# Moving one batch's loads and row tiles in a tuned attention and feed-forward kernel

## The chip, the cores and the metric

The kernel runs on one core of one Trainium2 chip. The metric is device time in microseconds (us), the median of several executions. Engines: PE is TensorE's matmul stream, PEld its weight loads, DVE is VectorE, ACT is ScalarE, POOL is GpSimd, SP is SyncE. A traced span is about 2 us shorter than the device time of the same run.

## The reference, cut to what matters

```python
def _attn_ref(q, k, v, g_norm):            # q, k, v: 8 batches x 8 heads x 576 x 64, float32
    kv = np.einsum('bhsd,bhse->bhde', k, v)
    out = np.einsum('bhsd,bhde->bhse', q, kv)
    rms = np.sqrt(np.mean(out * out, axis=-1, keepdims=True) + 1e-06)
    return out / rms * g_norm

def _moe_ref(x, w_in, w_out, alpha):       # x: 4608 x 512, w_in: 512 x 2048, w_out: 2048 x 512
    h = x @ w_in
    g = np.maximum(h, 0.0) + alpha * np.minimum(h, 0.0)
    return g @ w_out
```

The second takes the first's output, rows of all batches one after the other. The two matmuls of the feed-forward layer are most of the work; the attention of the next batches has to be ready in time.

## The kernel before: the parts that matter

The 4608 rows are worked in nine blocks of 512 (`w` = 0 to 8). A block has 16 units (`g`): four matmuls into a PSUM bank h_ps, an evacuation by ACT (m_sb) and DVE (gt), and four matmuls y_ps of the block before. From batch 2 on, attention runs in row tiles inside the block loop: matmul otm_ps, square and sum, rg on POOL, xrow on DVE, and a DMA transpose into xm, the input of the block. Only when q, k and v of a batch have landed can its kv product run on PE.

```python
    def phase_steps(w):                     # what of attention goes into the units of block w - 1
        ...
        kv_at = {NB_PE: 3, NB_PE + 1: 6, NB_PE + 2: 2}.get(w, 0)      # NB_PE = 2
        n = {NB_PE: 5, NB_PE + 1: 2}.get(w, 0)                        # empty units first
        steps += [([], [], []) for i in range(n)]
        ...
    for w in range(1, NW):
        steps = phase_steps(w + 1)
        for g in range(NF):
            ...
            m1_group(w, g, (H_POOL + [S_POOL])[g % 4] if w == 1 else None)
            ...
            if (w, g) == (1, 2):
                gate = const_p.tile([1, 1], FP16, name="gate")
                nc.gpsimd.tensor_copy(out=gate[:], in_=qtms[2][0:1, 0, 0:1])
                load(3, "q")
            if (w, g) == (1, 9):
                regroup(3, "q", eng=nc.gpsimd)
            if (w, g) == (1, 12):
                nc.gpsimd.tensor_copy(out=gate[:], in_=xm(2)[0:1, 0, W - 1 : W])
                load(3, "k")
                load(3, "v")
                transpose_q(3)
            if (w, g) == (2, 3):
                regroup(3, "k")
```

The two `gate` copies are there only to make POOL wait: the first until batch 2's transposed q has landed, the second until the last row of block 2's input has. So the loads behind them do not run beside those transposes.

## Time and profile before

| | us |
|---|---|
| median of three runs before the prediction | 298.36 (298.17 to 298.56) |
| traced span | 296.5 |
| mean granted clock of that run | 0.992 |
| PE busy | 283.5 |

Two rows of the page cut the span into 40 slices of 7.4 us. The first is the granted TensorE clock in tenths, the second the busy share of the DMA engines:

```profile
PEclk9999999999979999999999999999999999999999
DMA  7999999967999852992499459915212411112232
```

One slice of the clock stands out, the twelfth (81.5 to 89 us); the DMA engines are full up to 59 us, slacker in the next two slices, and full again from 74 us on, where k and v of batch 3 still move (issued from 69.7 us). The other lines are in the prediction.

### The profile page before, as it was taken

How to read it: one execution, taken by the hardware profiler on the slowest of the kernel's cores; microseconds unless marked ns; L12 is line 12 of the kernel's file. 1: busy time of each engine (PE TensorE's matmuls, PEld its weight loads, DVE VectorE, ACT ScalarE, POOL GpSimd, SP SyncE). 2: the span in 40 equal slices, each digit the busy share in tenths (PEclk: the TensorE clock that was granted, in tenths of full speed). 3: DMA queues.
4: the chain of work that ended last, by engine and by line, in shares of the span. 5: the costliest groups of instructions: out<-in, count | busy, mean ns of one | idle time of the engine just before them, and what ended most of it. 6: DMA issues, size and time to landing. Idle time of an engine off the chain costs nothing.

```text
span 296.5 us, 4288 instructions
## 1 busy us (share of the span) xinstructions
PE 283.5 (96%) x1551; PEld 139.2 (47%) x1551; DVE 169.8 (57%) x262; ACT 152.6 (51%) x297; POOL 98.0 (33%) x110
## 2 busy tenths in 40 slices
PE   5989999998979999999999999999999999999994
PEld 2554454543444454445444544454445444444443
DVE  4569847686557577446844684468447744444300
ACT  1459457584428456446744654467447544444311
POOL 9833411374155524542654274324002200000000
PEclk9999999999979999999999999999999999999999
DMA  7999999967999852992499459915212411112232
GB/s 90 181 206 203 200 205 199 186 116 148 179 138 192 134 96 63 171 235 48 99 147 217 90 90 170 237 36 100 53 35 46 89 35 38 35 46 50 49 71 71
DMA packets 66228, 35.54 MB, mean 120 GB/s; under 512 B 32784, under 2 KB 61728, under 8 KB 66208
## 3 DMA queue, kind: packets, MB, share of 16 engines
q0 software_dynamic: 29664, 18.35, 45.7%
q1 hardware_dynamic: 36384, 16.80, 27.5%
q8 instruction: 12, 0.20, 0.3%
q10 hardware_dynamic: 160, 0.13, 0.2%
q14 instruction: 8, 0.07, 0.1%
HBM read 36.71 MB, written 9.44 MB: 156 GB/s over the span
## 4 chain that ended last, share of the span: by engine, by line
PE 84%; DMA 7%; POOL 3%; DVE 2%; issue 1%; ACT 1%; POOLq 0%; DVEq 0%
PE h_ps L478 38%; PE y_ps L505 36%; DMA vst<-in_v_dram 4%; PE kv_ps L245 3%; DMA w_in_sb<-in_moe_w_in_dram 3%; PE otm_ps L397 2%; PE yb L505 1%; PE ya L505 1%; PE yd L505 1%; PE yc L505 1%; DMA xm<-xrow 1%; POOL kst L97 1%; POOL kst L102 1%; POOL vst L97 1%; POOL qst L97 0%
## 5 line engine op out<-in xcount | busy, mean ns | idle before, releaser
L487 DVE SCALAR_TENSOR_TENSOR gt<-m_sb,beta_sb,h_ps 128x512 f16<-128x512 f32 x144 | 105.6, 744 | 77.2 <-ACT m_sb L485 76.6
L485 ACT ACTIVATE m_sb<-h_ps 128x512 f32<-128x512 f32 x144 | 85.4, 597 | 89.9 <-PE h_ps L478 88.6
L505 PE MATMUL y_ps<-w_out_sb,gt 128*128 128x512 f16 (+1 forms) x528 | 129.7, 374 | 0.0
L478 PE MATMUL h_ps<-xm,w_in_sb 128*128 128x512 f16 x448 | 115.1, 379 | 1.0 <-DVE gt L487 1.0
L505 PEld LDWEIGHTS <-gt 128*128 128x128 f16 x592 | 57.8, 98 | 64.9 <-issue 0.9
L478 PEld LDWEIGHTS <-w_in_sb 128*128 128x128 f16 x584 | 55.8, 98 | 63.1 <-issue 3.4
L421 POOL TENSOR_TENSOR rg<-ss,g_all 128x512 f32<-128x512 f32 (+1 forms) x30 | 31.3, 1042 | 86.0 <-ACT ss L419 81.1
L478 PE MATMUL h_ps<-xt,w_in_sb 128*128 128x512 f16 (+1 forms) x136 | 30.6, 366 | 1.0 <-DMA w_in_sb<-in_moe_w_in_dram 0.5
L515 ACT COPY y_sb<-y_ps 128x512 f32<-128x512 f32 (+1 forms) x32 | 18.4, 576 | 15.9 <-PE y_ps L505 15.9
L409 DVE TENSOR_REDUCE ss<-sqm_sb 128x8 f32<-128x512 f32 (+1 forms) x30 | 20.5, 682 | 9.8 <-ACT sqm_sb L403 9.8
L430 DVE TENSOR_TENSOR xrow<-otm_ps,rg 128x512 f16<-128x512 f32 (+1 forms) x30 | 20.5, 682 | 3.6 <-POOL rg L421 3.6
L403 ACT ACTIVATE sqm_sb<-otm_ps 128x512 f32<-128x512 f32 (+1 forms) x30 | 17.7, 591 | 6.3 <-PE otm_ps L397 6.3
L112 POOL COPY ksb<-kst 128x2560 f16<-128x2560 f16 x5 | 11.6, 2321 | 15.2 <-DMA kst<-in_k_dram 15.2
L112 POOL COPY qsb<-qst 128x2560 f16<-128x2560 f16 x5 | 11.6, 2317 | 10.7 <-issue 10.7
L245 PE MATMUL kv_ps<-vst,ksb 128*128 128x128 f16 x160 | 11.1, 227 | 2.4 <-DMA vst<-in_v_dram 2.3
L397 PEld LDWEIGHTS <-qtm 128*128 128x128 f16 x120 | 9.2, 98 | 7.1
L245 PEld LDWEIGHTS <-ksb 128*128 128x128 f16 x160 | 10.0, 102 | 5.3 <-DVE gt L487 2.7
L416 ACT ACTIVATE ss<-ss,eps_t 128x8 f32<-128x8 f32 (+1 forms) x30 | 9.0, 301 | 6.0 <-DVE ss L409 5.6
L204 PE MATMUL warm_ps<-warm,mask 128*128 128x512 f16 x25 | 8.5, 481 | 3.3 <-DVE eps_t L146 3.3
L397 PE MATMUL otm_ps<-kv_sb,qtm 128*128 128x128 f16 x120 | 11.6, 219 | 0.0
L513 DVE COPY y_sb<-y_ps 128x256 f32<-128x256 f32 x1 | 0.4, 425 | 13.4 <-PE y_ps L505 13.4
L102 POOL DMA_DIRECT2D vst<-in_v_dram x9 | 6.4, 708 | 3.3 <-DMA w_in_sb<-in_moe_w_in_dram 1.9
(76 smaller groups left out, 137.5 us busy)
## 6 DMA issues: line engine op xcount, KB each, us to landing
out_dram<-y_sb SPq DMA_DIRECT2D x70, 128.0 KB, 2.4
kst<-in_k_dram POOLq DMA_DIRECT2D x7, 320.0 KB, 8.5
qst<-in_q_dram POOLq DMA_DIRECT2D x7, 320.0 KB, 4.8
vst<-in_v_dram POOLq DMA_DIRECT2D x7, 320.0 KB, 10.6
w_in_sb<-in_moe_w_in_dram POOLq DMA_DIRECT2D x4, 512.0 KB, 10.2
w_out_sb<-in_moe_w_out_dram POOLq DMA_DIRECT2D x4, 512.0 KB, 15.0
kst<-in_k_dram POOLq DMA_DIRECT2D x7, 256.0 KB, 9.6
qst<-in_q_dram POOLq DMA_DIRECT2D x7, 256.0 KB, 6.6
```

Of the source, the lines that this page charges most:

```text
L112: (eng or nc.vector).tensor_copy(out=bufs[b % NBUF][nm][:, :, h0:h1, :].rearrange("p t h d -> p h t d"), in_=stages[b % NBUF][nm][:, h0:h1],)
L245: nc.tensor.matmul(out=kv_ps[:, j - j0, :], lhsT=ks(t), rhs=vs(t), start=(t == 0), stop=(t == NT - 1),)
L397: nc.tensor.matmul(out=ot_ps[:, 2 * j : 2 * j + 2, :], lhsT=qtms[b][:, t * NPAIR + j, :], rhs=kvs[b, j], start=True, stop=True,)
L403: nc.scalar.activation(out=sq[0:n], in_=ot_ps[0:n], func=AF.Square)
L409: nc.vector.tensor_reduce(out=ss[0:n], in_=sq[0:n], op=ALU.add, axis=mybir.AxisListType.X,)
L421: nc.gpsimd.tensor_tensor(out=rg[0:n], in0=ss[0:n].unsqueeze(2).to_broadcast([n, H, D]), in1=g_all[0:n].unsqueeze(1).to_broadcast([n, H, D ...
L430: nc.vector.tensor_mul(out=x[0:n], in0=ot_ps[0:n], in1=rg[0:n])
L478: nc.tensor.matmul(out=h_ps[:, cols], lhsT=w_in_blk(c, g), rhs=xt_of(w, c)[:, cols], start=(c == 0), stop=(c == NC - 1 and cols.stop == W),)
L485: nc.scalar.activation(out=m_sb[:], in_=h_ps[:], func=AF.Relu, scale=-1.0)
L487: nc.vector.scalar_tensor_tensor(out=gt[:], in0=m_sb[:], scalar=beta_sb[:, g : g + 1], in1=h_ps[:], op0=ALU.mult, op1=ALU.add,)
L505: nc.tensor.matmul(out=y[:], lhsT=gts[w, g][:, a * P : (a + 1) * P], rhs=w_out_blk(g)[:, cols], start=(g == 0), stop=(g == NF - 1),)
L515: nc.scalar.copy(out=y_sb[:, cols], in_=y[:])
```

## The change

Its intent: batch 3's kv product should not wait for v. k goes ahead of the row transposes, together with q, and only v stays behind the gate. The tiles start a unit sooner, which opens the gate sooner. k is regrouped on POOL instead of DVE. Smaller pieces: in block 0 one sum of squares goes ahead of four matmuls, three more y matmuls go ahead of each of two other sums of squares, and of its four PSUM banks block 1 now takes last the one that the tail uses (the last 128 rows of batch 1, which fall into block 2). To regroup is to copy a loaded tensor into the order in which PE reads it.

```diff
-        n = {NB_PE: 5, NB_PE + 1: 2}.get(w, 0)
+        n = {NB_PE: 4, NB_PE + 1: 2}.get(w, 0)
...
+    half_ssq(0, O2)
     for g in range(4):
-        if g == 2:
-            half_ssq(0, O2)
         m1_mm(first[g], 0, g, (0,))
...
-    ahead(9, 11)
+    ahead(9, 12)
     ssq_mm(1, 3, S_POOL)
...
-    ahead(13, 14)
+    ahead(13, 15)
     norm(1, 3)
     step_tail_ssq(0, S_POOL)
...
-            m1_group(w, g, (H_POOL + [S_POOL])[g % 4] if w == 1 else None)
+            m1_group(w, g, [H_POOL[0], H_POOL[2], S_POOL, H_POOL[1]][g % 4] if w == 1 else None)
...
                 load(3, "q")
-            if (w, g) == (1, 9):
+                load(3, "k")
+            if (w, g) == (1, 8):
                 regroup(3, "q", eng=nc.gpsimd)
-            if (w, g) == (1, 12):
+            if (w, g) == (1, 11):
                 nc.gpsimd.tensor_copy(out=gate[:], in_=xm(2)[0:1, 0, W - 1 : W])
-                load(3, "k")
                 load(3, "v")
                 transpose_q(3)
-            if (w, g) == (2, 3):
-                regroup(3, "k")
+                regroup(3, "k", eng=nc.gpsimd)
```

(The other `ahead` calls only close the gaps that these leave.)

## The prediction

> **What bounds the kernel now.** I read the busy shares first, then what TensorE (PE) waited for, then the chain of waits around the one long wait, then a clean unit of the same kind to price it, then the granted clock, and last the order of time on PE before it. The page's busy shares and the shares of the chain:
>
> ```profile
> PE 283.5 (96%) x1551; PEld 139.2 (47%) x1551; DVE 169.8 (57%) x262; ACT 152.6 (51%) x297; POOL 98.0 (33%) x110
> ...
> PE 84%; DMA 7%; POOL 3%; DVE 2%; issue 1%; ACT 1%; POOLq 0%; DVEq 0%
> ```
>
> PE is busy 283.5 of a span of 296.5 us, so at most 13 us can come from waits; the number of matmuls does not change. Which waits are they? PE's own list (total us, times, longest):
>
> ```profile
> PE warm_ps L204 <- DVE eps_t L146: 3.3, 1, 3.3
> PE kv_ps L245 <- DMA vst<-in_v_dram: 2.3, 1, 2.3
> PE h_ps L478 <- DVE gt L487: 1.0, 1, 1.0
> PE h_ps L478 <- DMA w_in_sb<-in_moe_w_in_dram: 0.5, 1, 0.5
> ```
>
> The first is the start-up and is not touched. The second and third are the change's targets: batch 3's kv product waits for v, and block 2's first matmul waits. The chain from 60 to 90 us (start, duration, what):
>
> ```profile
> 65.97 0.60 DVE xrow L430
> ...
> 66.69 2.43 DMA xm<-xrow
> ...
> 69.70 0.72 POOL kst L97
> 70.42 0.68 POOL kst L102
> ...
> 71.34 0.45 POOL vst L97
> ...
> 72.02 11.21 DMA vst<-in_v_dram
> 83.23 0.14 issue
> 83.36 1.97 PE kv_ps L245 x20
> 85.34 1.71 PE y_ps L505 x4
> 87.04 0.98 PE h_ps L478 x4
> ```
>
> Read it downwards: the last row transpose of block 2's input lands at 66.69 + 2.43 = 69.12; only then does GpSimd (POOL) issue k and, behind it, v; v's second half lands at 83.23; PE begins kv at 83.36. For the price, the same three groups in block 3, where nothing waits:
>
> ```profile
> 107.28 0.86 PE h_ps L478 x4
> 108.14 1.12 PE kv_ps L245 x20
> 109.25 0.86 PE y_ps L505 x4
> ```
>
> and the stretches after the wait (length, PE, PEld, DVE, ACT, POOL busy with counts, PEclk, DMA share, GB/s):
>
> ```profile
> 82.00:84.00 2.00, 0.64 (x10) 0.67 (x11) 1.47 (x3) 0.81 (x2) 2.00 (x3) 0.94 0.43 102
> 84.00:86.00 2.00, 2.00 (x16) 1.45 (x15) 1.62 (x3) 0.00 (x0) 2.00 (x4) 0.50 0.76 68
> ```
>
> The granted clock fell to 0.50 after the wait. So the wait costs 2.28 us of idleness plus slow matmuls: 1.97 − 1.12 = 0.85, 1.71 − 0.86 = 0.85, 0.98 − 0.86 = 0.12. Together **4.10 us**.
>
> Last, PE in order of time in block 1 and at the start of block 2:
>
> ```profile
> 53.80 1.28 PE L245 MATMUL kv_ps<-vst,ksb 128*128 128x128 f16 x20
> ...
> 57.29 0.39 PE L397 MATMUL otm_ps<-kv_sb,qtm 128*128 128x128 f16 x4
> ...
> 69.26 1.02 PE L478 MATMUL h_ps<-xm,w_in_sb 128*128 128x512 f16 x4 [0.95 <-DVE gt L487]
> ```
>
> The 0.95 us is put down to DVE's gt, but the bank that this matmul writes (h0) was freed about 67.8, as I count the gt back from the last of block 1, while xm landed at 69.12: the real releaser is the transpose. The batch-2 kv at 53.80 is a pin too: batch 2's last v load was issued at 39.60 and took 14.1 us, so it landed at 53.7.
>
> **What the Trainium skill says.** "TensorE: Matmul & The Clock Gate", section "What's actually happening": an idle array drops to half clock and needs sustained work to get it back, with a free-running window of about 3.4 us. The trace agrees on the half (0.50) and on a recovery within some 3 us; here an idle stretch of only 2.28 us was enough, shorter than that window. The 0.95 us wait did not trip it (1.00 throughout). "DMA: Bandwidth & Descriptors", section "Queues, rings and completion order": each DMA engine takes turns between the queues that have work, a packet at a time, so GpSimd's loads and SyncE's transposes slow each other. The trace agrees: a transpose xm<-xrow lands in 2.4 us when no load is in flight (64.1 to 66.7), in 4.9 and 6.8 us beside batch 4's loads (issued at 93.2 and 83.7). "SBUF — State Buffer", section "Who interferes with whom": vector copies in a two-port mode and GpSimd lock each other out of one port pair. k's regrouping moves from DVE to POOL; the trace shows POOL's copy of q (64.44 to 66.76) beside multiplies of 0.68 and 0.74 us, their usual durations, so I count nothing.
>
> **The change part by part.**
>
> Part 1, k ahead. k (two issues, 0.72 + 0.68 us) leaves the slot behind the transposes and goes right behind q, about 57.84 to 59.2. Behind the gate only v is left, so v is issued 1.40 + 0.23 = 1.6 us sooner after the gate, and half as many bytes are in the queue. Before, k + v + the transposition of q (0.59 + 0.59 + 0.66 MB as written, plus 0.26 MB of output) took 69.7 to 83.2. Without k's 0.59 MB at the 175 to 200 GB/s of those stretches, 3 to 3.4 us go. So v lands near 83.2 − 1.6 − 3.2 ≈ 78.4 if the gate opens as before, about 77.3 if it opens a unit sooner. PE is ready for it at 80.06 + 0.86 = 80.92 (about 80.1 if block 2 starts sooner). Margin about 2.5 us: the wait and its slow clock go whole, **−4.1 us**. The margin hardly depends on the gate, because PE's start of block 2 and v's issue hang on the same transpose.
>
> Part 2, k's regrouping from DVE (0.83 us, after a 2.7 us wait for k) to POOL (2.32 us). Neither bounds; at about 71 to 73.4 POOL is free and ksb is ready seven us before kv. **0**. It also frees POOL's later issues of batch 4, which waited behind that DVE wait.
>
> Part 3, the tiles a unit sooner. The first tile's matmuls move from 57.29 to about 56.21, just after batch 2's transposed q lands (48.33 + 7.6 = 55.93) and kv is masked (55.81). ACT and DVE then carry the three tiles at their own pace (about 1.3 to 1.8 us each), so the last xrow ends about 1.15 to 1.3 us sooner, 65.3, and a quiet transpose would land at about 67.9. PE's work of block 1 ends at 68.31. Thus up to −0.95 us.
>
> Against this: k's 0.59 MB now runs in that stretch. q's halves landed at 61.5 and 63.25. From 58 to 63 about 0.74 MB were still to move; with k 1.33 MB at about 200 GB/s end near 65 to 66.5. That overlaps the first transpose and part of the second, but little of the third. I take a landing at 68.3 and a start of block 2 at about 68.45: **−0.8 us**.
>
> Part 4, block 0 and the fills: the first sum of squares goes ahead of block 0's first matmuls (which wait 0.5 us for weights anyway) and more y matmuls fill the waits of 0.17 and 0.2 us before two others. Worth some 0.3 and 0.4 us locally. But all of it is before 53.80, and there v of batch 2 lands at 53.7 out of a DMA stretch that moved 196 to 205 GB/s from 42 to 52. PE only arrives earlier and waits longer. **0**.
>
> Part 5, bank order h0, h2, s, h1. It lets block 1's second unit avoid the tail's bank; h2 instead waits for the copy of ya, which ends about 50.2. Also before 53.80, so **0**. Its price is that unit 15 leaves h1, which block 2's unit 1 needs about 1.73 us after the start, near 70.0; DVE's last gt of block 1 ended at 69.86, and should now end nearer 69.3. Just in time.
>
> Sum: −4.1 − 0.8 = −4.9; 298.36 − 4.9 = 293.5 us. After kv nothing in the list of waits is left, and block 3's input was landed by about 100 against a need at 103.38, so the gain is carried to the end.
>
> **The rivals.** First, the transposes collide with k. For it: 4.9 and 6.8 us beside loads, and batch 2's transposition of q took 7.6 us against 5.0 quiet. Against it: tiles are sooner and k is short. If the last lands at 70 to 70.5 instead, block 2 starts 0.9 to 1.2 us later than now: about 295.3. If it waits over 2 us the clock may fall again, and nearly all is lost: 297 to 298. Second, v still sets the wait: if the transposition of q, now sooner, takes the bandwidth, v lands at 81 or later and a short wait without the slow clock stays: 294 to 295. For it: that transposition took 10.8 us beside k and v. Third, the pin at 53.7 is looser than I think and part 4's 0.5 us survive: 293.0; together with the whole 0.95, 292.6. Fourth, h1 or the backlog of ACT and DVE holds block 2's second unit for some tenths: 293.9.
>
> **Range and chances.** Centre 293.5; the good ends reach 292.6, a collision 295.3. I say 292.5 to 295.3. Faster by over 2% means below 292.39, which needs −6.0 us; the two waits with all their cost hold 4.1 + 0.95 = 5.05, and part 4 would have to survive whole as well: 0.07. Slower by over 2% needs 6 us of new waits: 0.01. Within 2%: 0.92.
>
> **What would show it.** Right: PE's list has no vst wait above 0.3 us, the clock stays 1.00 from 80 to 90, kv takes 1.12 us, and k lands before 67. Batch 2's kv still begins within 0.15 us of 53.80 with a longer wait before it. The last transpose of block 2 lands between 67.9 and 68.8. Wrong: transposes xm<-xrow around 63 to 68 that take over 4 us, a dip of the clock about 69 to 72, kv of batch 2 before 53.5, or any wait of over 1 us on PE after 85.

## The result, and the profile after

The changed kernel took 294.12 us (median of four runs, 293.58 to 294.48), the kernel before 298.46 us (four runs, 298.17 to 298.88). The ratio is 0.9852, 95% interval 0.9832 to 0.9871. A ratio is the mean time of one kernel's runs over that of the other's in the same rounds, so it is not quite the ratio of the medians. The spans are 292.0 and 296.5 us. Clock and DMA rows of the changed kernel's page, now in slices of 7.3 us:

```profile
PEclk9999999999999999999999999999999999999999
DMA  7999999999999916991699179934212311212133
```

The fall of the clock is gone, and the two slacker slices of the DMA row are filled, because k is loaded there now. PE's list of waits, the three that answer to those before:

```profile
PE h_ps L478 <- DMA xm<-xrow: 0.5, 1, 0.5
PE ssq_ps L327 <- ACT sq_sb L267: 0.5, 1, 0.5
PE kv_ps L245 <- DMA vst<-in_v_dram: 0.4, 1, 0.4
```

The 2.3 us wait for v is gone. The 0.4 us that bears the same name is another one, at batch 2's kv. The 0.5 us before a sum of squares (ssq_ps) is in block 0, in the place of the 0.5 us wait for weights. The wait at block 2 fell from 0.95 to 0.5 us, and is now put down to the transpose. The chain of waits over the same stretch:

```profile
66.36 2.44 DMA xm<-xrow
68.81 0.14 issue
68.94 1.02 PE h_ps L478 x4
...
80.77 1.12 PE kv_ps L245 x20
81.89 0.86 PE y_ps L505 x4
```

Where v and its slow matmuls stood there is PE alone: kv takes 1.12 us, the clean price. POOL in order of time shows the new place of the loads:

```profile
58.21 0.70 POOL L97 DMA_DIRECT2D kst<-in_k_dram  x1
58.88 0.71 POOL L102 DMA_DIRECT2D kst<-in_k_dram  x1
...
68.93 0.18 POOL L701 COPY gate<-xm 1x1 f16<-1x1 f16 x1 [2.88 <-DMA xm<-xrow]
70.17 0.74 POOL L97 DMA_DIRECT2D vst<-in_v_dram  x1 [1.06 <-PE h_ps L478]
70.89 0.70 POOL L102 DMA_DIRECT2D vst<-in_v_dram  x1
```

By the trace's times to landing, k's halves were there at 65.9 and 67.3, and v's at 76.6 and 77.9, 2.7 us before PE wanted it at 80.61.

Four stretches of PE account for the span. Each is the difference of two start times:

| stretch | before | after | difference |
|---|---|---|---|
| start to batch 2's kv | 53.80 | 54.15 | +0.35 |
| from there to block 2 (69.26; 68.94) | 15.46 | 14.79 | −0.67 |
| from there to unit 7 of block 2 (86.84; 82.59) | 17.58 | 13.65 | −3.93 |
| from there to the end | 209.66 | 209.41 | −0.25 |

The sum is −4.5 us. The first row is where v of batch 2 landed: issued at the same time (39.61; 39.60), it took 14.4 us against 14.1. That is no loss shown to come from the change. Of the last row, 0.12 us are unit 7's slow first matmuls of before.

### The profile page after: what moved, and what is told of

The parts are those of the page before. It is cut to its first block, busy times and chain, and to the rows that moved or that the text cites. A ratio compares the mean times of both kernels' runs of the same rounds, so it can differ in the third digit from the quotient of the medians.

```text
span 292.0 us, 4287 instructions
## 1 busy us (share of the span) xinstructions
PE 281.5 (96%) x1551; PEld 138.2 (47%) x1551; DVE 169.0 (58%) x261; ACT 153.0 (52%) x297; POOL 100.4 (34%) x111
## 4 chain that ended last, share of the span: by engine, by line
PE 76%; DMA 17%; DVE 2%; POOL 2%; ACT 1%; issue 1%; POOLq 0%; DVEq 0%
PE y_ps L505 38%; PE h_ps L478 33%; DMA vst<-in_v_dram 5%; DMA w_in_sb<-in_moe_w_in_dram 5%; DMA w_out_sb<-in_moe_w_out_dram 4%; PE kv_ps L245 2%; PE otm_ps L397 2%; DMA kst<-in_k_dram 2%; DVE gt L487 1%; DMA xm<-xrow 1%; POOL w_in_sb L165 1%; DVE ss L409 1%; DVE xrow L430 1%; ACT sqm_sb L403 0%; POOL qst L97 0%
## 5 line engine op out<-in xcount | busy, mean ns | idle before, releaser
L112 POOL COPY ksb<-kst 128x2560 f16<-128x2560 f16 x6 | 14.0, 2326 | 15.5 <-DMA kst<-in_k_dram 15.5
L245 PE MATMUL kv_ps<-vst,ksb 128*128 128x128 f16 x160 | 10.4, 219 | 0.9 <-DMA vst<-in_v_dram 0.4
L245 PEld LDWEIGHTS <-ksb 128*128 128x128 f16 x160 | 9.4, 98 | 3.7 <-POOL ksb L112 0.9
```

Source lines behind the costliest of these rows:

```text
L112: (eng or nc.vector).tensor_copy(out=bufs[b % NBUF][nm][:, :, h0:h1, :].rearrange("p t h d -> p h t d"), in_=stages[b % NBUF][nm][:, h0:h1],)
L245: nc.tensor.matmul(out=kv_ps[:, j - j0, :], lhsT=ks(t), rhs=vs(t), start=(t == 0), stop=(t == NT - 1),)
```

## The experiments

Twelve runs of ten different kernels, six executions each, in three sets, each set on its own chip with 11 executions of the kernel before. My theory: k ahead removes v's wait with its slow clock, the tiles win a little at block 2, and everything ahead of batch 2's kv is swallowed there. Rivals: the gate's earlier opening carries the gain; or the fills do; or the collision of k with the transposes eats much of it.

**The yardstick.** The changed kernel once more.

> The changed kernel once more, as the yardstick of this set: 294.1 us, ratio to before 0.985. Block 2 starts about 14.8 us after batch 2's kv, batch 3's kv without a wait.

Measured: 294.26 us, ratio 0.9866 (0.9819 to 0.9912); batch 2's kv to block 2 took 15.11 us here. One of its six runs had a clock of 0.994, though the trace of another shows no wait at batch 3's kv; that run was not traced. The kernel before, however, scattered from 295.97 to 300.24 us. More on that below.

**Loads alone.** To the kernel before:

```diff
                 load(3, "q")
+                load(3, "k")
...
-                load(3, "k")
                 load(3, "v")
                 transpose_q(3)
-            if (w, g) == (2, 3):
-                regroup(3, "k")
+                regroup(3, "k", eng=nc.gpsimd)
```

> The kernel before with k of batch 3 loaded right behind q and regrouped on GpSimd behind v; tiles, fills and banks as before. My theory: v's wait with its slow clock goes whole (-4.1 us), and k meets the transposes later, so block 2 starts at most 0.5 us later than before: 294.3 to 295 us. Rival (the gain comes from the gate opening a unit sooner): little gain, 297 us or more, and a vst wait of over 1 us stays.

Measured: 294.50 us, ratio 0.9877. Nearly the whole gain is in the order of the loads. Block 2 began 15.52 us after batch 2's kv, before 15.46: with the tiles at their old place k (landed 66.0 and 67.4) hurts the last transpose by almost nothing.

**Tiles alone.** To the kernel before: `n` from 5 to 4, gate and q's regrouping one unit sooner with them, k and v both still behind the gate.

> The kernel before with only the tiles a unit sooner (and the gate and q's regrouping with them); k and v both behind the gate. My theory: the 0.95 us wait at block 2 goes (quiet transposes), the gate opens about 1.1 us sooner and so does v, but PE gets to kv 0.9 sooner as well: the vst wait stays at about 2.1 us with its slow clock, so -0.9 to -1.1 us: 297.3 us. Rival (the gate's time is what counts): the vst wait falls by 1 us or more and the clock stays up: 295 us or less.

Measured: 296.68 us, ratio 0.9943 (0.9895 to 0.9991). The trace agrees with my theory and not with the rival: the wait at block 2 is gone, and the wait for v stays. PE's kv in order of time, and the stretch after it:

```profile
82.60 1.42 PE L245 MATMUL kv_ps<-vst,ksb 128*128 128x128 f16 x20 [2.17 <-DVE xrow L430]
```

```profile
84.00:86.00 2.00, 2.00 (x7) 0.65 (x5) 0.69 (x1) 0.00 (x0) 1.28 (x2) 0.50 1.14 152
```

The bracket names DVE, but v's second half landed at 82.48 (issued 71.37, 11.1 us), so it is v again. Counted from batch 2's kv (54.22 in this trace, 53.80 before), PE was ready 1.07 us sooner and v landed 1.17 us sooner: opening the gate sooner hardly helps a wait when PE's own start hangs on the same transpose. The median is 0.6 us below what I expected: only three of the six runs (297.3 to 297.8 us, clock 0.993 to 0.994) had the slow clock; the other three, at 0.999 to 1.000, took 295.1 to 296.0 us.

**No fills.** The changed kernel with block 0, the `ahead` calls and the bank order as before.

> The changed kernel with block 0's sum of squares, the fills of y matmuls and the bank order put back. My theory (all of it lies ahead of batch 2's kv, which waits for v's landing at 53.7 to 54.0): the same time as the changed kernel within 0.2 us. Rival (the fills carry): 0.4 to 0.6 us slower.

Measured: 294.18 us, against 294.26 us for the changed kernel beside it. These pieces are worth nothing that the runs can show. Where they went is seen in PE's order of time, in the kernel before and then in the first trace of the changed kernel (units 0, 1 and 3 of block 1):

```profile
49.48 1.03 PE L478 MATMUL h_ps<-xt,w_in_sb 128*128 128x512 f16 x4
50.57 1.02 PE L478 MATMUL h_ps<-xt,w_in_sb 128*128 128x512 f16 x4
...
52.73 1.03 PE L478 MATMUL h_ps<-xt,w_in_sb 128*128 128x512 f16 x4
```

```profile
49.13 1.03 PE L478 MATMUL h_ps<-xt,w_in_sb 128*128 128x512 f16 x4
...
50.56 1.02 PE L478 MATMUL h_ps<-xt,w_in_sb 128*128 128x512 f16 x4 [0.18 <-ACT y_sb L515]
...
52.72 1.03 PE L478 MATMUL h_ps<-xt,w_in_sb 128*128 128x512 f16 x4
```

Block 1 began 0.35 us sooner, but unit 1 waited for the copy that frees h2, the bank that the new order gives it, and PE came to batch 2's kv at the same time as before. In all ten traces with fills and new order unit 1 begins 1.42 to 1.43 us after unit 0, in the four without them 1.09 us.

**The pin.** If they are swallowed by v of batch 2, taking that away should give something back. Edit, with a wrong result (each of q, k and v is loaded in a long part of 320 KB and a short one of 256 KB; the short part of v is never loaded):

```diff
-    load_batch(2)
+    load(2, "q")
+    load(2, "k")
+    load_part(2, "v", True)
```

> The changed kernel with only the long part of batch 2's v loaded (wrong result on purpose), so that v is no longer what batch 2's kv waits for. My theory (that landing swallows what block 0 and the fills gain): the wait of 0.3 to 0.4 us before batch 2's kv goes and the time falls by 0.3 to 0.6 us. Rival (no pin): the same time.

Measured: 293.26 us, against 293.65 us for the changed kernel on that chip. The wait before batch 2's kv is gone from the trace. The sign and size are as expected, but the intervals of the two ratios overlap (0.9847 to 0.9907; 0.9864 to 0.9927), so the trace carries this more than the time does. Nor does the edit only take the pin away: with 256 KB less to load, batch 2's transposed q landed sooner, k of batch 3 was issued at 56.23 instead of 57.57 us, and block 2 followed batch 2's kv after 14.56 us instead of 14.77. The pin itself is seen in the changed kernel:

```profile
54.15 1.28 PE L245 MATMUL kv_ps<-vst,ksb 128*128 128x128 f16 x20 [0.41 <-DMA vst<-in_v_dram]
```

It does not bind in every run: in the yardstick's trace PE came later, and kv began at 54.40 without a wait.

**The collision.** The changed kernel without any load of batch 3's k (wrong result).

```diff
                 load(3, "q")
-                load(3, "k")
```

> The changed kernel without any load of batch 3's k (wrong result on purpose). If k ahead collides with the row transposes: the three transposes land in 2.4 us each instead of 4.5, 3.3 and 2.4, SyncE issues the last 0.4 to 0.5 us sooner, block 2 hardly waits: 0.4 to 0.6 us faster than the changed kernel, 293.7 us. Rival (the last transpose comes after k's end, so nothing is lost): the same within 0.15 us.

Measured: 293.39 us, ratio 0.9878, on another chip than the yardstick's, so I read the trace. SP's three transposes, in the changed kernel and then without k:

```profile
63.37 4.21 SPq L435 DMA_TRANSPOSE xm<-xrow  x3
```

```profile
62.62 3.82 SPq L435 DMA_TRANSPOSE xm<-xrow  x3
```

With k they landed after 4.5, 3.3 and 2.4 us, without it after 2.4 us each. The third is never slow itself; it is issued later, because SP holds its queue for the first (1.6 us instead of 1.2). Without k, block 2 began 14.38 us after batch 2's kv (67.79 − 53.41) and did not wait; with k 14.79. Tiles alone, with a right result and quiet transposes, has the same 14.38 us (68.60 − 54.22). So the sooner tiles are worth 15.46 − 14.38 = 1.08 us, and the collision takes 0.41 of it in this trace of the changed kernel, 0.39 and 0.73 in its two others (14.77 and 15.11 us); in the last, SP held its queue 1.9 us for the first transpose.

**Half of k.** Could one have both? Only k's long part ahead, the short part behind the gate before v, k regrouped on DVE.

```diff
                 load(3, "q")
-                load(3, "k")
+                load_part(3, "k", True)
...
+                load_part(3, "k", False)
                 load(3, "v")
                 transpose_q(3)
-                regroup(3, "k", eng=nc.gpsimd)
+            if (w, g) == (2, 3):
+                regroup(3, "k")
```

> The changed kernel with only the long part of batch 3's k ahead of the transposes, the short part behind the gate before v, and k regrouped on VectorE in block 2 as before. If the collision costs some tenths and v's margin (2.7 us in the changed kernel) bears the 256 KB in front of it: v lands near 79.5, no wait, block 2 starts 0.3 us sooner: 294.0 us. Rival (k's short part or v comes too late): a wait at batch 3's kv returns, 295 to 297 us, some runs with a clock below 0.995.

Measured: 293.89 us, ratio 0.9889, no wait for v at batch 3's kv. That looked like a gain, but the chip was another one. So it ran again beside the changed kernel.

> The changed kernel beside the next three on one chip: 294.2 us; no run with a clock below 0.995, while some runs of the kernel before have 0.992 to 0.994 and are some 2 us longer than its others.

Measured: 293.65 us, ratio 0.9896; no run with a clock below 0.997, while two of the kernel before had 0.992.

> Half of k ahead, once more, now on the changed kernel's chip. If it takes away part of the collision: 0.2 to 0.4 us faster than the changed kernel. Rival: it was the chip, and the two are equal within 0.1 us.

Measured: 293.79 us, ratio 0.9893. The rival was right: no gain. The wait at block 2 was 0.29 us in one trace and 0.47 us in the other, the changed kernel's 0.48 us. As k's regrouping was on DVE here, this also speaks for its move to POOL being worth nothing, though half of k was in another place too.

**Batch 2's kv one y matmul later**, on top of half of k:

```diff
-            steps[kv_at][1].append(...)
+            steps[kv_at][2 if w == NB_PE else 1].append(...)
```

> Half of k ahead, and batch 2's kv product moved behind the one y matmul of its unit, which fills 0.22 us of PE's wait for v: 0.2 us faster than half of k alone, 293.7 us. Rival (the tiles behind it move by the same 0.2 us and the row transposes with them, so the wait at block 2 grows): no gain.

Measured: 293.81 us, 293.04 to 296.28; nothing gained. The wait for v there was 0.30 us in its trace. One run of 296.28 us at clock 1.000 stays unexplained. No version was found that beats the changed kernel.

**The clock.** Why did the kernel before scatter so? The result lists the mean granted clock of every run. In the traces a fall to half lasts 3.4 us (below); of 296 us that lowers the mean by some 0.006, so the runs can be told apart, if roughly:

| kernel (wait at batch 3's kv in its trace) | runs with clock 0.991 to 0.994, mean us | runs with clock 0.996 or more, mean us |
|---|---|---|
| before, all three sets (2.28 us in the first trace) | 9, 298.87 | 24, 296.73 |
| tiles alone (2.17) | 3, 297.50 | 3, 295.49 |
| the changed kernel, two sets (none) | 1, 295.09 | 11, 293.97 |

So the slow clock comes in some executions and not in others, and those with it are about 2 us longer in the first two rows. The split is by the clock of a whole run; where a fall lies only a trace shows, and the one of tiles alone and the first of the kernel before have it right after the wait. To see what decides, v was held back in the changed kernel by repeating k's regrouping ahead of it:

```diff
+                for _ in range(3):          # 4 in the second kernel
+                    regroup(3, "k", eng=nc.gpsimd)
                 load(3, "v")
                 transpose_q(3)
-                regroup(3, "k", eng=nc.gpsimd)
```

> The changed kernel with v of batch 3 held back behind three copies of k's regrouping on GpSimd (7 us, the result is the same): v is issued near 76.2 and lands near 82.4, kv waits some 1.5 to 2 us. If the clock's fall is a matter of where the wait lies in a free-running window: some runs at 0.993 and some at 0.998 or more, about 2 us apart, 296 to 298 us. Rival (the idle time alone decides): all runs alike.

Measured: 298.15 us. Four runs had a clock of 0.992 to 0.994 (mean 298.35 us), two 0.997 and 0.999 (297.31 us), so 1.0 us apart and not 2.

> The same with four copies: v is issued near 78.5 and lands near 84.7, kv waits about 4 us. If the window is about 3.4 us, as the page has it, every run falls (clock 0.990 to 0.994): 294.2 + 4 + 2 = 300 us. Rival (the fall is luck at any length): runs of both kinds.

Measured: 299.40 us, and all six runs at 0.991 to 0.994. PE's kv in order of time in the two kernels, with the wait in the bracket:

```profile
83.30 1.37 PE L245 MATMUL kv_ps<-vst,ksb 128*128 128x128 f16 x20 [2.47 <-DMA vst<-in_v_dram]
```

```profile
84.32 1.64 PE L245 MATMUL kv_ps<-vst,ksb 128*128 128x128 f16 x20 [3.57 <-DMA vst<-in_v_dram]
```

Where a traced wait was 2.2 to 2.5 us, some executions of the kernel fell; where it was 3.57 us, all six did. The clock in the stretches after the 2.47 us wait:

```profile
84.00:86.00 2.00, 2.00 (x15) 1.07 (x13) 0.69 (x1) 0.00 (x0) 0.00 (x0) 0.59 1.42 159
86.00:88.00 2.00, 2.00 (x6) 0.71 (x5) 0.00 (x0) 0.00 (x0) 0.00 (x0) 0.56 1.61 172
```

A mean of 0.59 is 1.64 us at half clock, 0.56 is 1.76 us: 3.4 us together, from about 84.36, 1.1 us after PE had begun again. The other three falls, worked out in the same way, last 3.4 us too and begin 0.4 to 1.0 us after PE's restart (before 83.74, tiles alone 83.60, four copies 85.08). In the 3.4 us before each fall PE had been idle for 2.2 to 2.7 us. The Trainium skill, "TensorE: Matmul & The Clock Gate", section "What's actually happening", says that the window of about 3.4 us is free-running and does not start with the kernel. The 3.4 us of the four falls, and their start only after PE was busy again, agree with it. If some 2.2 idle us in one window are enough, a wait of that length lowers the clock where it lies in one window and not where it straddles two; that would explain runs of both kinds. It is a reading of four traces, not shown: all four are of runs that fell, so the rival that v landed sooner and the wait was shorter in the runs that were spared stays open. Nor does "always" follow for 3.57 us, which two windows could share; six of six is a count.

## Why the prediction was right

*v's wait goes whole (−4.1 us).* The mechanism held: k ahead alone gives 294.50 us, v lands 2.7 us before it is wanted (I had put the margin at about 2.5), kv takes 1.12 us, and the stretch that held the wait is 3.93 us shorter. v was issued only 0.9 us sooner after the gate (1.24 us behind it, before 2.10) and not 1.6: POOL waited 1.06 us, by the profile for block 2's first matmuls. The margin bore it. One term was taken as certain and is not: the 1.82 us of slow matmuls. They were in the traced run, but in only 9 of 33 later runs of the kernel before is the clock low. Without them the idle 2.28 us and block 2's share are left: against the runs of before without a fall, 296.73 − 294.07 (all twelve later runs of the changed kernel, over different chips) = 2.7 us. The first comparison's 4.3 us is high, as all four runs of before lay at 298.2 to 298.9 us, the level of the fallen ones; of these only the traced one's clock is known (0.992). That the sum came out is so in part luck: 298.36 us happened to be a base at that level, from which the slow clock could be subtracted.

*Tiles a unit sooner (−0.8 us).* Measured −0.67 us in the first trace, −0.35 and −0.69 in the repeats (15.11 and 68.33 − 53.56 = 14.77 against 15.46). Without the collision it is 1.08 us, where I had 0.95; the collision takes 0.39 to 0.73 us of it, where I had 0.15. I had thought of the third transpose's own data; it was SP's queue, held 0.4 us longer by the first. The sign that I had called wrong was there, a transpose of over 4 us (the first, 4.5), and k's second half landed at 67.3, not before 67. The rival in which it costs 0.9 us or more did not come.

*Fills, first sum of squares, bank order, k's regrouping (0).* Right by time (294.18 against 294.26 us). The mechanism was so only in part. The 0.3 and 0.4 us of part 4 were there: block 1 began 0.35 us sooner in a run whose first kv product had begun 0.35 us later (10.68 against 10.33). But the 0.35 us were lost at once, at the copy that frees h2, and not at the pin: PE did not arrive earlier at batch 2's kv. Part 5 had named that copy, but not that it takes back part of part 4's gain; whether the old bank order would have kept it is open, as no run has the fills with that order. The kv began at 54.15 and not within 0.15 us of 53.80, with a wait of 0.41 us (the list's vst wait was to stay within 0.3), because v landed at 54.02 in that run; the pin moves with the load. For the regrouping on its own there was no run; half of k, which kept it on DVE, was no slower.

*h1 just in time.* Block 2's second unit began 1.73 us after the first (70.67 after 68.94), with no wait.

*The centre.* 293.5 us against 294.12 us: 0.13 of the 0.6 us are block 2's smaller gain, and 0.35 us in the traced run is the later kv of batch 2, which no part of the change is shown to cause. The good end of the range was added wrongly: 298.36 − 4.1 − 0.95 − 0.5 is 292.8, not 292.6.

## What to carry to other kernels

When one transpose both starts a stage and opens the gate for the loads that this stage will wait for, bringing it forward moves both ends; what shortens the wait is taking bytes out from behind the gate. Before counting a gain ahead of a stage, look for a landing time in between that PE cannot pass. And when a wait is followed by slow matmuls in one trace, look at the clock of the other runs before counting that price in full.

## What the Trainium skill lacked or had wrong

- "TensorE: Matmul & The Clock Gate": the section "Why this matters for your kernels" warns of idle gaps of more than about 3 us. Here gaps of 2.17 to 2.47 us in the traces went with a lower clock in some executions (9 of 33, 3 of 6, 4 of 6) and one of 3.57 us in all of six. The page has the free-running window, but does not say that a shorter gap can cost a share of the runs, here 1.0 to 2.1 us each.
- "DMA: Bandwidth & Descriptors": the section "Queues, rings and completion order" has the engines take turns between queues, and the trace agrees in direction (a transpose lands in 2.4 us quiet, in 3.3 to 4.5 us beside k). It lacks that the issue itself gets longer: SP held its queue 1.6 us instead of 1.2 for a transpose beside loads, which delayed a third one that was not slow itself.
- No page has what a load from POOL costs beside such transposes as a whole: 0.39 to 0.73 us for k's two issues here, and 0.06 us (15.52 against 15.46) with the tiles at their old place.
